# First q piece by SP's queue, doubled natural q and k tiles, a DMA-sharing schedule model and quotas of 10, 10, 10, 8, 7: sliding-window attention followed by a cosine-gated feed-forward layer

## The chip, the cores and the metric

The kernel runs on one core of one Trainium2 chip. The metric is the device time of one execution in microseconds (us). The kernel before was tuned already: 317.22 us, the median of three runs (317.15 to 318.24).

## The reference, cut to what matters

```python
batch, n_heads, seq, head_dim = (8, 8, 576, 64)          # q, k, v: float32
scores = scale * np.matmul(q, k.transpose(0, 1, 3, 2))
mask = (rel >= 0) & (rel < 128)                          # sliding window
scores = np.where(mask, scores + bias[None], -1e9)       # bias: ALiBi slopes
attn = softmax(scores); x = attn @ v                     # -> 4608 tokens x 512
h = x @ w_in                                             # 512 x 2048
g = h * np.cos(h)
return g @ w_out                                         # 2048 x 512
```

## The kernel before: the parts that matter

The kernel records operations, with what they read and write. A list scheduler with a model of durations then puts each engine's operations in an order. **The chip's time does not enter that model**: the model only decides the order. Waits on semaphores come from the recorded dependences.

Attention is cut into 72 units, 9 per batch: 8 of 256 queries of a head pair, and a tail. The feed-forward layer is cut into 9 chunks of 512 tokens. Phase c does the first matmul of chunk c, then `QUOTA[c]` attention units, then the second matmul of chunk c. The last units are thus far ahead of the chunk that uses them.

```python
QUOTA = [9, 9, 12, 12, 8, 8, 5]
...
# in schedule(), for an operation that issues a DMA: each queue has a wire of its own
if o.dma is not None:
    wire[e] = max(wire[e], st + 2300) + o.lat
    o.end = max(wire[e], st + o.occ + 1400) + 500
...
nat = {"q": sb("qnat", [128, NBLK, H, D]), "k": sb("knat", [128, NBLK, H, D])}   # one tile each
...
def load_nat(which, src, b):        # from batch 2 on: natural rows, 5 DMAs on GpSimd's queue
    ...
    op("pool", fns, w=[("nat", which)], dma=f"ldn{which}", occ=4400, lat=5500)

def dma_transposes(b):              # natural rows -> transposed rows, 2 DMAs on SP's queue
    for which in ("q", "k"):
        ...
        op("sp", fns, r=[("nat", which)] + ..., w=[("tr", which, b % 2)], ..., occ=2500, lat=6500)
...
# a finished unit is transposed into xT by PE if the next chunk needs it, else by a DMA from SP
first = (S * u[0] + (512 if u[1] == "t" else 256 * u[2])) // CH
after.append((first > phase + 1, u, ub, n))       # True: x_dma, False: x_pe
...
load_qk("q", q, 0, 0)               # all on GpSimd's queue, cast to bf16 by the DMA
load_qk("k", k, 0, 0)
distances()
identity()
load_qk("q", q, 0, 1)
load_qk("k", k, 0, 1)
constants()
load_v(0)
masks()
...
for u in range(4):
    load_w_in(u)
...
while next_t < B and done >= 9 * (next_t - 1):     # after the attention of a phase
    load_v(next_t)
    ...
    dma_transposes(next_t)
    next_t += 1
    if next_t < B:
        load_nat("q", q, next_t)
        load_nat("k", k, next_t)
```

Names: PE is TensorE, ACT ScalarE, DVE VectorE, POOL GpSimd, SP SyncE. `qrows` and `krows` are the rows of batches 0 and 1, `qnat` and `knat` the natural rows of later batches, `qt` and `kt` the transposed ones.

The softmax here doesn't subtract the row's maximum and nothing guards it: scores larger than these inputs give would overflow.

## Time and profile before

| | before |
|---|---|
| time, median of 3 (and of 6 in the comparison) | 317.22 us (317.75) |
| span of the profiled execution | 316.6 us; that execution took 318.35 us |
| PE busy | 303.8 us |
| matmuls that transpose x | 66 |
| PE wait for batch 4's transposed k | 1.3 us |

From the page of the kernel before (busy times; mean busy share of the DMA engines in tenths, 40 slices; shares of the chain that ended last):

```profile
span 316.6 us, 6278 instructions
...
PE 303.8 (96%) x2466; PEld 155.9 (49%) x2466; DVE 189.3 (60%) x453; ACT 202.9 (64%) x292; POOL 95.7 (30%) x123
...
DMA  6999999999999999999999994132013001201112
...
PE 84%; DMA 10%; POOL 4%; SPq 1%; issue 1%; ACT 0%; POOLq 0%; ACTq 0%
```

PE is the bound: there is little to win but its waits. The DMA engines are busy until slice 24 (190 us). The waits of PE (waiting line, what it waited for: total us, times, longest):

```profile
PE ps L432 <- DMA qrows<-in_q_dram: 5.8, 2, 5.4
PE ps L476 <- DMA kt<-knat: 1.3, 1, 1.3
PE ps L485 <- DVE kt L448: 0.9, 1, 0.9
...
PE ps L432 <- DMA krows<-in_k_dram: 0.4, 1, 0.4
```

The 5.4 us are the start. The 1.3 us are the one wait over 0.4 us after the first 15 us (one of 0.5 us, left out above, ends at 13.99). The chain of waits that leads to it (start us, duration us, what):

```profile
94.40 1.73 POOL knat L341 x2
96.13 6.68 DMA knat<-in_k_dram
102.83 1.87 SPq L350
...
104.74 8.81 DMA kt<-knat
...
113.59 0.41 PE ps L476 x16
```

Natural k is loaded until 102.8 us, transposed by a DMA until 113.55, and PE starts on it at 113.59. The start in the timeline (start, duration, engine, line, operation, and in brackets the idle time before and what ended it):

```profile
5.40 1.07 PE L432 MATMUL ps<-ident,qrows 128*64 128x128 bf16 x16 [5.40 <-DMA qrows<-in_q_dram]
6.91 1.07 PE L432 MATMUL ps<-ident,krows 128*64 128x128 bf16 x16 [0.44 <-DMA krows<-in_k_dram]
8.85 0.83 PE L485 MATMUL ps<-qt,kt 64*128 64x256 bf16 x8 [0.88 <-DVE kt L448]
```

### The profile page before, as it was taken

The page shows a single profiled execution, that of the slowest core. Times are in us where ns is not written, and L with a number is a line of the kernel's source. Part 1 is how long each engine was busy: PE and PEld are TensorE (multiplying, and loading weights), DVE is VectorE, ACT ScalarE, POOL GpSimd, SP SyncE. Part 2 cuts the span into 40 slices and gives each one's busy share as a digit, 9 for nine tenths or more (in the row PEclk, how much of TensorE's full clock was granted, in tenths as well). Part 3 has the DMA queues.
Part 4 walks back from the last instruction along what each step waited for, and adds up shares of the span by engine and source line. Part 5 has one row for each costly group of instructions (what it writes and reads, how often), then busy time and mean ns, then how long its engine had stood idle before and what let it go on. Part 6 is the DMA issues. An engine that isn't in the chain of part 4 may idle for free.

```text
span 316.6 us, 6278 instructions
## 1 busy us (share of the span) xinstructions
PE 303.8 (96%) x2466; PEld 155.9 (49%) x2466; DVE 189.3 (60%) x453; ACT 202.9 (64%) x292; POOL 95.7 (30%) x123
## 2 busy tenths in 40 slices
PE   2799999999999989999999999999999999999996
PEld 2577755444544554455444444454445444444444
DVE  2798858676685777858795856574753461363000
ACT  5896865886698766867787766667674553362211
POOL 8997140078357554564507200000000000000000
PEclk9999999999999999999999999999999999999999
DMA  6999999999999999999999994132013001201112
GB/s 95 178 206 210 205 161 192 154 154 133 172 175 165 164 157 158 171 168 183 155 126 122 163 111 85 66 77 58 18 56 73 33 0 48 86 0 68 66 72 94
DMA packets 144620, 37.82 MB, mean 119 GB/s; under 512 B 134224, under 2 KB 139600, under 8 KB 144592
## 3 DMA queue, kind: packets, MB, share of 16 engines
q0 software_dynamic: 99616, 18.36, 77.1%
q1 hardware_dynamic: 44976, 19.08, 29.8%
q8 instruction: 19, 0.31, 0.4%
q14 instruction: 9, 0.07, 0.1%
HBM read 36.70 MB, written 9.44 MB: 146 GB/s over the span
## 4 chain that ended last, share of the span: by engine, by line
PE 84%; DMA 10%; POOL 4%; SPq 1%; issue 1%; ACT 0%; POOLq 0%; ACTq 0%
PE ps L746 36%; PE ps L675 34%; DMA qrows<-in_q_dram 5%; PE ps L485 4%; DMA kt<-knat 3%; PE ps L570 2%; DMA knat<-in_k_dram 2%; PE ps L698 2%; PE ps L573 1%; POOL vp L331 1%; PE ps L720 1%; PE ps L639 1%; PE ps L432 1%; POOL w_inb L361 1%; PE ps L557 1%; PE ps L476 1%
## 5 line engine op out<-in xcount | busy, mean ns | idle before, releaser
L746 PE MATMUL ps<-w_outb,gT 128*128 128x512 bf16 x560 | 134.2, 380 | 0.0
L675 PE MATMUL ps<-xT,w_inb 128*128 128x512 bf16 x512 | 115.9, 379 | 0.0
L684 DVE TENSOR_TENSOR gT<-ps,cos 128x512 bf16<-128x512 f32 x128 | 81.0, 685 | 47.8 <-PE ps L746 39.0
L680 ACT ACTIVATE cos<-ps,halfpi 128x512 f32<-128x512 f32 x128 | 80.6, 688 | 31.1 <-PE ps L746 13.4
L746 PEld LDWEIGHTS ps<-w_outb,gT 128*128 128x128 bf16 x560 | 51.6, 98 | 56.4 <-issue 1.7
L675 PEld LDWEIGHTS ps<-xT,w_inb 128*128 128x128 bf16 x512 | 48.4, 97 | 57.4 <-DVE gT L684 4.5
L515 ACT ACTIVATE p<-ps 128x768 bf16<-128x768 f32 (+1 forms) x64 | 55.4, 915 | 22.0 <-PE ps L485 19.0
L539 DVE TENSOR_TENSOR p<-p,emask 128x512 bf16<-128x512 bf16 (+1 forms) x96 | 41.2, 460 | 8.0 <-ACT p L515 7.6
L752 ACT ACTIVATE ob<-ps 128x512 f32<-128x512 f32 x26 | 15.6, 599 | 38.7 <-PE ps L746 38.6
L331 POOL DMA_DIRECT2D vp<-in_v_dram x40 | 33.8, 882 | 15.3 <-issue 9.3
L341 POOL DMA_DIRECT2D qnat<-in_q_dram x30 | 25.3, 877 | 38.8 <-DMA qt<-qnat 38.8
L341 POOL DMA_DIRECT2D knat<-in_k_dram x30 | 25.3, 879 | 25.7 <-DMA kt<-knat 23.3
L611 DVE TENSOR_TENSOR xnat<-ps,rec 128x256 bf16<-128x256 f32 x64 | 24.4, 420 | 0.5
L485 PE MATMUL ps<-qt,kt 64*128 64x128 bf16 (+1 forms) x320 | 19.1, 245 | 1.7 <-DVE kt L448 0.9
L570 PEld LDWEIGHTS ps<-vp,p 128*128 128x128 bf16 x256 | 15.7, 97 | 7.4 <-issue 3.5
L570 PE MATMUL ps<-vp,p 128*128 128x65 bf16 x256 | 18.2, 194 | 0.4 <-issue 0.3
L485 PEld LDWEIGHTS ps<-qt,kt 64*128 64x128 bf16 x320 | 11.5, 96 | 12.8 <-issue 5.3
L609 DVE RECIPROCAL rec<-ps 128x4 f32<-128x4 f32 x64 | 8.2, 167 | 15.3 <-PE ps L573 14.9
L573 PE MATMUL ps<-vp,p 128*128 128x65 bf16 x192 | 17.0, 193 | 0.0
L698 PE MATMUL ps<-xT,w_inb 128*128 128x256 bf16 x128 | 16.2, 273 | 0.1
L573 PEld LDWEIGHTS ps<-vp,p 128*128 128x128 bf16 x192 | 13.3, 97 | 0.5
L754 DVE COPY ob<-ps 128x512 f32<-128x512 f32 x9 | 6.2, 691 | 12.2 <-PE ps L746 12.2
(52 smaller groups left out, 173.1 us busy)
## 6 DMA issues: line engine op xcount, KB each, us to landing
out_dram<-ob SPq DMA_DIRECT2D x35, 256.0 KB, 2.2
vp<-in_v_dram POOLq DMA_DIRECT2D x32, 128.0 KB, 9.0
qnat<-in_q_dram POOLq DMA_DIRECT2D x24, 128.0 KB, 5.7
knat<-in_k_dram POOLq DMA_DIRECT2D x24, 128.0 KB, 5.8
w_inb<-in_moe_w_in_dram POOLq DMA_DIRECT2D x4, 512.0 KB, 10.4
w_outb<-in_moe_w_out_dram POOLq DMA_DIRECT2D x4, 512.0 KB, 22.6
qrows<-in_q_dram POOLq DMA_DIRECT2D x1, 576.0 KB, 15.5
krows<-in_k_dram POOLq DMA_DIRECT2D x1, 576.0 KB, 17.6
```

The costliest lines, as they stand in the source:

```text
L331: op("pool", [lambda e, t=t, rows=rows: e.dma_start(vp[b % 2][0:rows, t, :, 0:64], v[b, :, 128 * t:128 * t + rows, :].rearrange("h p d -> ...
L341: fns.append(lambda e, t=t, rows=rows: e.dma_start(nat[which][0:rows, t, :, :], src[b, :, 128 * t:128 * t + rows, :].rearrange("h p d -> p ...
L485: ins = e.matmul(ps[:, banks[x], c0:c1], keys_ap(b, x, pr, kc), query_ap(b, x, pr, qb, 128 * nb), start=True, stop=True)
L515: op("act", lambda e: e.activation(P[i][:, :, 0:hi], src_[:, :, 0:hi], ACTF.Exp, scale=0.125), w=held + [("P", i)], occ=920 if G else 691, ...
L539: op("dve", lambda e, p=p, m=m: e.tensor_tensor(p, p, m, ALU.mult), r=[("P", i), ("EM", h0), ("EM", h1)], w=[("P", i)] if n != 1 else [("P ...
L570: ins = e.matmul(o, P[i][:, x, d0:d0 + 128], V[:, kc, h, 0:65], start=True, stop=not two)
L573: ins = e.matmul(o, P[i][:, x, p0:p0 + 128], V[:, kc - 1, h, 0:65], start=False, stop=True)
L611: op("dve", lambda e: e.tensor_tensor(o, U[:, :, :, 0:64], rv[:, :, :, None].broadcast_to([128, 2, 2, 64]), ALU.mult), r=[("rec", n % 2)], ...
L675: op("pe", lambda e, kc=kc: e.matmul(ps[:, bank, :], w_in[:, kc, 128 * fc:128 * fc + 128], xT[:, kc, r0:r0 + CH], start=(kc == 0), stop=(k ...
L680: op("act", lambda e: e.activation(cosb[ci][:, :], ps[:, bank, :], ACTF.Sin, bias=halfpi[:, 0:1]), r=["halfpi"], w=[("B", bank), ("cos", c ...
L684: op("dve", lambda e: e.tensor_tensor(gT[gi][:, fc, :], ps[:, bank, :], cosb[ci][:, :], ALU.mult), r=[("cos", ci)], w=[("B", bank), ("g", ...
L746: op("pe", lambda e, t=t, fc=fc, bank=bank: e.matmul(ps[:, bank, :], gT[gi][:, fc, 128 * t:128 * t + 128], w_out[:, fc, :], start=(fc == 0 ...
```

## The change

Its intent: to start earlier by using SP's idle queue for the first q piece; to let the natural loads of a batch begin while those of the batch before are still being transposed; to tell the scheduler that both queues share the DMA engines; and to spread the attention units more evenly over the phases.

```diff
-                wire[e] = max(wire[e], st + 2300) + o.lat
+                other = "sp" if e == "pool" else "pool"
+                begin = max(wire[e], st + 2300)
+                both = min(o.lat, max(0, wire[other] - begin))
+                wire[e] = begin + o.lat + both
+                wire[other] += both
...
-        nat = {"q": sb("qnat", ...), "k": sb("knat", ...)}
+        nat = {w_: [sb(f"{w_}nat{i}", ...) for i in range(2)] for w_ in ("q", "k")}
...
-        QUOTA = [9, 9, 12, 12, 8, 8, 5]
+        QUOTA = [9, 9, 10, 10, 10, 8, 7]
...
+        def load_first_q():
+            op("sp", [lambda e: e.dma_start(obuf[:, 0:2, :], rows)], ..., dma="hwq", ...)
+            for y, eng in enumerate(("dve", "act")):     # cast the float halves to bf16
+                op(eng, ..., r=[("ob", y)], w=[("qB", "q", 0, y)], ...)
...
-            op("pool", fns, w=[("nat", which)], dma=f"ldn{which}", occ=4400, lat=5500)
+            op("pool", fns, r=[("tr", which, 0)] if b == 3 else [], w=[("nat", which, b % 2)],
+               dma=f"ldn{which}{b % 2}", occ=4400, lat=4500)
...   # modelled latencies: DMA transposes 6500 -> 4300 and 500 -> 450, stores 600 -> 750
-        load_qk("q", q, 0, 0)
+        load_first_q()
         load_qk("k", k, 0, 0)
...
-        load_v(0)
+        load_v(0, range(2))
+        load_w_in(0)
+        load_v(0, range(2, NBLK))
```

More of the change, by code (lines that the diff above doesn't have):

```diff
@@ L267, in bass_alibi_sliding__then__act_gcu_kernel @@
         qB = {"q": sb("qrows", [128, 2, 1152]), "k": sb("krows", [128, 2, 1152])}
-        nat = {"q": sb("qnat", [128, NBLK, H, D]), "k": sb("knat", [128, NBLK, H, D])}
+        nat = {w_: [sb(f"{w_}nat{i}", [128, NBLK, H, D]) for i in range(2)] for w_ in ("q", "k")}
         tr = {w_: [sb(f"{w_}t{i}", [128, 2560]) for i in range(2)] for w_ in ("q", "k")}
@@ L280, in bass_alibi_sliding__then__act_gcu_kernel @@
         NOB = 4
-        ob = [sb(f"ob{i}", [128, 512], F32) for i in range(NOB)]
+        obuf = sb("ob", [128, NOB, 512], F32)
+        ob = [obuf[:, i, :] for i in range(NOB)]
         rec = [sb(f"rec{i}", [128, 8], F32) for i in range(2)]
@@ L317, in piece_keys @@
         def piece_keys(which, b, n):
-            return [("qB", which, 0), ("qB", which, 1)] if b else [("qB", which, n)]
+            keys = [("qB", which, 0), ("qB", which, 1)] if b else [("qB", which, n)]
+            return keys + ([("qB", "q", 0, 0), ("qB", "q", 0, 1)] if which == "q" and n == 0 else [])
         def load_qk(which, src, b, n=0):
@@ L326, in load_qk @@
                w=piece_keys(which, b, n), dma=f"ld{which}{n}", occ=740, lat=159 * R)
+        def load_first_q():
+            t0, R, _ = PIECES[0][0]
+            rows = bass.AP(q.tensor, q[0].offset, [[64 * R, 32], [64 * S, H], [1, 64 * R]])
+            op("sp", [lambda e: e.dma_start(obuf[:, 0:2, :], rows)],
+               w=[("ob", 0), ("ob", 1)], dma="hwq", occ=60, lat=500)
+            for y, eng in enumerate(("dve", "act")):
+                o = qB["q"][:, y, 0:512]
+                op(eng, (lambda e, o=o, y=y: e.tensor_copy(o, ob[y])) if y == 0 else
+                   (lambda e, o=o, y=y: e.activation(o, ob[y], ACTF.Copy)),
+                   r=[("ob", y)], w=[("qB", "q", 0, y)], occ=(340, 450)[y], lat=(420, 560)[y],
+                   pri=3)
         def load_v(b, order=range(NBLK)):
@@ L341, in load_nat @@
                 fns.append(lambda e, t=t, rows=rows: e.dma_start(
-                    nat[which][0:rows, t, :, :],
+                    nat[which][b % 2][0:rows, t, :, :],
                     src[b, :, 128 * t:128 * t + rows, :].rearrange("h p d -> p h d")))
-            op("pool", fns, w=[("nat", which)], dma=f"ldn{which}", occ=4400, lat=5500)
+            op("pool", fns, r=[("tr", which, 0)] if b == 3 else [], w=[("nat", which, b % 2)],
+               dma=f"ldn{which}{b % 2}", occ=4400, lat=4500)
         def dma_transposes(b):
@@ L351, in dma_transposes @@
                         t[:, 0:4, :, :].rearrange("p c k t -> p (c k) t"),
-                        nat[which][:, 0:4, :, :].rearrange("p c h d -> p (c h d)")),
+                        nat[which][b % 2][:, 0:4, :, :].rearrange("p c h d -> p (c h d)")),
                     lambda e, t=t, which=which: e.dma_start_transpose(
                         t[:, 4, :, 0:64],
-                        nat[which][0:64, 4, :, :].rearrange("p h d -> p (h d)")),
+                        nat[which][b % 2][0:64, 4, :, :].rearrange("p h d -> p (h d)")),
                 ]
-                op("sp", fns, r=[("nat", which)] + ([("ktail", b % 2)] if which == "k" else []),
-                   w=[("tr", which, b % 2)], dma=f"tr{which}{b % 2}", occ=2500, lat=6500)
+                op("sp", fns, r=[("nat", which, b % 2)] + ([("ktail", b % 2)] if which == "k" else []),
+                   w=[("tr", which, b % 2)], dma=f"tr{which}{b % 2}", occ=2500, lat=4300)
         def load_w_in(u):
@@ L658, in x_dma @@
                    r=[("xtl", b % 2)], w=[k_ for p_ in range(NPAIR) for k_ in xkeys(p_, t0, 64)],
-                   dma=f"xt{b % 2}", occ=1250, lat=500)
+                   dma=f"xt{b % 2}", occ=1250, lat=450)
                 return
@@ L663, in x_dma @@
                 xT[:, pr, t0:t0 + 256].rearrange("p (r t) -> p r t", r=2), xnat[n % NX][:, :])],
-               r=[("xnat", n % NX)], w=xkeys(pr, t0, 256), dma=f"x{n % NX}", occ=1250, lat=500)
+               r=[("xnat", n % NX)], w=xkeys(pr, t0, 256), dma=f"x{n % NX}", occ=1250, lat=450)
         ccount = [0]
@@ L752, in moe2 @@
                    {"act": lambda e, bank=bank, oi=oi: e.activation(
-                       ob[oi][:, :], ps[:, bank, :], ACTF.Copy),
-                    "dve": lambda e, bank=bank, oi=oi: e.tensor_copy(ob[oi][:, :], ps[:, bank, :])},
+                       ob[oi], ps[:, bank, :], ACTF.Copy),
+                    "dve": lambda e, bank=bank, oi=oi: e.tensor_copy(ob[oi], ps[:, bank, :])},
                    w=[("B", bank), ("ob", oi)], occ={"act": 490, "dve": 606},
@@ L758, in moe2 @@
                 op("sp", [lambda e, oi=oi, row=row: e.dma_start(out[row:row + 128, :],
-                                                                ob[oi][:, :])],
-                   r=[("ob", oi)], dma=f"st{oi}", occ=60, lat=600)
+                                                                ob[oi])],
+                   r=[("ob", oi)], dma=f"st{oi}", occ=330, lat=750)
         ucount = [0]
@@ L809, in bass_alibi_sliding__then__act_gcu_kernel @@
             qk_transposes(0, "k", n, 0, UB)
-        for u in range(4):
+        for u in range(1, 4):
             load_w_in(u)
```

## The prediction

> **What bounds the kernel.** TensorE (PE). The page gives PE 303.8 us of a 316.6 us span (96%) and a chain that ended last that is 84% PE, 10% DMA, 4% POOL. In the timeline of PE, 512-column matmuls start 216 ns apart in both feed-forward stages throughout. The waits view lists under 10 us: 5.8 us for q rows (5.4 before anything has begun, 0.38 at 28.8 us), 0.4 for the first k rows, 1.4 for k copies, and one steady stall, 1.3 us at 113.6 us, for batch 4's transposed k. So the change can win only at the start and at that stall; all else is PE work.
>
> **Start.** Before: POOL issues q at 1.32 us (0.82 us) and k at 2.15; they land at 5.36 and 6.87; the first scores start at 8.85. After: SP issues q, POOL issues k first, 0.8 us earlier, and all its later loads too. The Trainium skill ("DMA: Bandwidth & Descriptors", "Issuing engines are not separate DMA queues") says both queues share the same 16 engines, so the q bytes are not free; but they move before POOL's first bytes. I expect k landed near 5.5 us. New cost: two casts, an estimated 0.4 us on VectorE and 0.5 us on ScalarE, the latter after four mask exponentials (0.32 us each, from about 3.4 us): PE starts at about 5.3 us, as before, but k's transposes follow without their wait. First scores near 8.3 us. ScalarE is busy nearly without a break from 9.4 to 20.5 us, so that shift is kept. Batch 1's rows (landing at 28.72 and 31.51 us, in an always full DMA queue) land 0.8 to 1.5 us earlier, so the 0.38 us wait mostly goes. Worth 0.8 us in all.
>
> **Batch 4 stall.** The chain of waits shows k loads issued at 92.7 us, after batch 3's k transposes landed (92.1), landed at 102.8, transposed by 113.55. With two natural tiles these loads go out some 8 to 15 us earlier, and batch 4's first use comes later (10 units, not 12, in that phase). The stall goes: 1.3 us. POOL's waits for q and k transposes (38.8 and 23.3 us) shrink by more than half; that alone gains nothing.
>
> **Cost.** The new quotas make 7 more units be transposed on PE instead of by DMA (instruction order: 66 to 80 matmuls). A pair costs PE 0.11 us: 0.8 us more. Switches between score and other matmuls stay 38 groups. Fewer units in the fullest phases save perhaps 0.3 us of short waits for exponentials.
>
> **Sum.** -0.8 -1.3 -0.3 +0.8 = -1.6 us: 315.6 us. Range 313.7 to 317.2. Faster by over 2%: 0.02; within 2%: 0.96; slower: 0.02.
>
> **What would show it.** Right: first scores at 8.0 to 8.5 us; no PE wait over 0.3 us after 35 us; 80 identity transposes of x; PE busy 303 to 304 us. Wrong: k landing after 6.5 us (SP's q crowding it out); the ScalarE cast holding PE past 5.7 us; batch 2's transposes (landed 69.0, used 70.5 before: the tightest) late by sharing DMA; a new wait in phases 5 and 6, which got more units.
>
> **What would make it wrong.** Loads running ahead may slow the DMA transposes (4 to 10 us each, DMA busy 90% up to 190 us) enough to stall batch 2 or 3; then 317 to 319 us. If the earlier start carries through whole (1.5 us), 314.5.

## The result

The changed kernel took 318.39 us at the median of six runs (317.75 to 319.08), the kernel before in the same rounds 317.75 (317.15 to 318.6). The ratio is 1.0021, with a 95% interval of 0.9998 to 1.0045: the same time, and outside the predicted range of 313.7 to 317.2. The two profiled executions, 318.38 and 318.35 us, are also alike: after the change PE was busy 1.1 us longer and idle about as much less. All ratios here are the mean time of one kernel's fast runs over that of the other's fast runs of the same rounds, so not quite the ratio of the medians. Executions over 1.5% slower than the fastest of the same kernel are left out of the means.

The page of the changed kernel, the lines that answer to those above:

```profile
span 316.5 us, 6268 instructions
...
PE 304.9 (96%) x2480; PEld 155.9 (49%) x2480; DVE 188.5 (60%) x448; ACT 209.5 (66%) x306; POOL 95.1 (30%) x122
...
DMA  7999999999999999999999894320012001201112
...
PE 62%; DMA 18%; POOL 11%; SPq 6%; issue 1%; ACT 0%; POOLq 0%; ACTq 0%
```

PE is as full as before, with 1.1 us more of busy time. The chain that ended last now runs through DMA, POOL and SP for a third of the span. The waits of PE:

```profile
PE ps L454 <- ACT qrows L344: 5.8, 1, 5.8
PE ps L507 <- DVE kt L470: 0.9, 1, 0.9
PE ps L498 <- DMA kt<-knat: 0.6, 1, 0.6
```

The stall for batch 4's k is still there, and PE starts 0.36 us later than before. The chain that leads to the stall:

```profile
79.58 18.01 DMA qnat<-in_q_dram
...
97.60 4.98 SPq L372
...
104.59 7.36 SPq L372
...
112.00 6.59 DMA kt<-knat
...
118.63 0.41 PE ps L498 x16
```

The natural loads were issued 8.5 us (q) and 12.4 us (k) earlier than before, as forecast. Yet the last of q's took 18.0 us to land, the large transposes of q and k then took SP 5.0 and 7.4 us to issue, and k landed transposed at 118.58 us, five microseconds later than in the trace before. The start, in the timeline:

```profile
5.04 0.63 ACT L344 ACTIVATE qrows<-ob 128x512 bf16<-128x512 f32 x1 [0.17 <-DMA ob<-in_q_dram]
...
5.76 1.06 PE L454 MATMUL ps<-ident,qrows 128*64 128x128 bf16 x16 [5.76 <-ACT qrows L344]
...
6.58 1.09 PE L454 MATMUL ps<-ident,krows 128*64 128x128 bf16 x16
...
8.55 0.82 PE L507 MATMUL ps<-qt,kt 64*128 64x256 bf16 x8 [0.88 <-DVE kt L470]
```

SP issued q at 0.81 us, but it landed only at 5.01; the two casts took 0.62 and 0.63 us where I had put 0.4 and 0.5 (the trace of before has ScalarE copies of 128x512 at 0.57 and 0.60 us). First scores came 0.30 us earlier than in this trace of before, not 0.55. Both traces happen to be late at the start: in a second trace of the changed kernel (e13) q landed at 4.73 us, PE started at 5.43 and first scores at 8.23. The transposes of x on PE, in the groups of instructions before:

```profile
L639 PE MATMUL ps<-ident,xnat 128*128 128x128 bf16 x66 | 8.8, 222 | 0.3
```

and after:

```profile
L661 PE MATMUL ps<-ident,xnat 128*128 128x128 bf16 x80 | 11.0, 222 | 0.0
```

POOL's waits are where the doubled tiles show. Before, its longest two:

```profile
POOL qnat L341 <- DMA qt<-qnat: 38.8, 5, 18.0
POOL knat L341 <- DMA kt<-knat: 23.3, 5, 11.7
```

and after, it waits for the attention to free v tiles instead:

```profile
POOL vp L351 <- PE ps L595: 37.8, 5, 13.3
POOL qnat L361 <- DMA qt<-qnat: 18.4, 1, 18.4
```

### The profile page after: what moved, and what is told of

Its sections match the earlier page's. It is cut to its first block, busy times and chain, and to the rows that moved or that the text cites. A ratio compares the mean times of both kernels' runs of the same rounds, so it can differ in the third digit from the quotient of the medians.

```text
span 316.5 us, 6268 instructions
## 1 busy us (share of the span) xinstructions
PE 304.9 (96%) x2480; PEld 155.9 (49%) x2480; DVE 188.5 (60%) x448; ACT 209.5 (66%) x306; POOL 95.1 (30%) x122
## 4 chain that ended last, share of the span: by engine, by line
PE 62%; DMA 18%; POOL 11%; SPq 6%; issue 1%; ACT 0%; POOLq 0%; ACTq 0%
PE ps L768 28%; PE ps L697 26%; DMA qnat<-in_q_dram 14%; SPq L372 6%; POOL vp L351 4%; POOL qnat L361 3%; PE ps L507 2%; DMA qt<-qnat 2%; DMA kt<-knat 2%; PE ps L592 2%; POOL knat L361 1%; PE ps L742 1%; POOL w_outb L389 1%; PE ps L595 1%; POOL w_inb L383 1%
## 5 line engine op out<-in xcount | busy, mean ns | idle before, releaser
L706 DVE TENSOR_TENSOR gT<-ps,cos 128x512 bf16<-128x512 f32 x128 | 81.9, 686 | 42.2 <-PE ps L768 29.8
L702 ACT ACTIVATE cos<-ps,halfpi 128x512 f32<-128x512 f32 x128 | 81.6, 688 | 29.2 <-PE ps L697 16.1
L774 ACT ACTIVATE ob<-ps 128x512 f32<-128x512 f32 x28 | 16.8, 599 | 41.8 <-PE ps L768 41.7
L361 POOL DMA_DIRECT2D qnat<-in_q_dram x30 | 25.6, 910 | 25.8 <-DMA qt<-qnat 18.4
L670 ACT ACTIVATE xT<-ps 128x256 bf16<-128x256 bf16 x27 | 9.9, 387 | 6.6 <-PE ps L661 6.5
## 6 DMA issues: line engine op xcount, KB each, us to landing
qnat<-in_q_dram POOLq DMA_DIRECT2D x24, 128.0 KB, 12.4
```

Of the source, the lines that this page charges most:

```text
L361: fns.append(lambda e, t=t, rows=rows: e.dma_start(nat[which][b % 2][0:rows, t, :, :], src[b, :, 128 * t:128 * t + rows, :].rearrange("h p ...
L702: op("act", lambda e: e.activation(cosb[ci][:, :], ps[:, bank, :], ACTF.Sin, bias=halfpi[:, 0:1]), r=["halfpi"], w=[("B", bank), ("cos", c ...
L706: op("dve", lambda e: e.tensor_tensor(gT[gi][:, fc, :], ps[:, bank, :], cosb[ci][:, :], ALU.mult), r=[("cos", ci)], w=[("B", bank), ("g", ...
```

## The experiments

The change has four parts: F (first q piece by SP, and the first w_in piece moved ahead of three v pieces), N (two natural tiles), M (the new model and latencies) and Q (quotas). Keeping none of them from the changed source gave exactly the instruction order of the kernel before, on every engine. All runs below were correct against the reference. A call is a set of kernels timed in the same rounds on one chip, the kernel before among them: e1 to e4, e5 to e8, e9 to e12, e13 to e15, e16 to e18. The runs of the kernel before scatter, so a comparison within one call says most. Medians are of all six runs. In its trace, e2 has the same instruction order as the kernel before on all five engines.

### One part alone, and all but one

**e1: F alone.** The only edit over the kernel before is part F of the diff.

> Kernel before plus the first part alone (first q piece by SP's queue into a float tile, two casts; first w_in piece moved ahead of three v pieces). Theory: in the changed kernel the start gained only 0.30 us (first scores 8.85 to 8.55) because q by SP landed no earlier than 5.01 and had to be cast; so 0.3 to 0.5 us faster here, stall of batch 4 (1.3 us) unchanged. Rival: the start was worth the predicted 0.8 us and something else ate it: first scores by 8.3 and 0.8 us faster.

Measured: 317.47 us (one slow run among the six, 322.31) against 318.17 for before, ratio 0.9989 (0.9934 to 1.0045). First scores at 8.24 us, and no wait for batch 4's k in this execution. The time can't tell 0.3 from 0.8 us. That the stall was gone was not foreseen: the first hint that the stall is not a fixed property of the kernel before.

**e2: N alone.** Two natural tiles and nothing else; old quotas, old model.

> Kernel before plus the doubled natural q and k tiles alone (old quotas, old model). Theory: the DMA engines are full, so loads issued earlier land hardly earlier and the loads of batch 5, now free to go, share the engines with batch 4's k transposes; those land at 113 to 119 us against 113.55 before, while their first use stays at 112 to 113 us: the stall stays at 1.3 us or grows to as much as 5 us; 0 to 4 us slower. Rival (my prediction): loads 8 to 15 us earlier, stall gone, 1.3 us faster.

Measured: 323.58 us, ratio 1.0173 (1.0129 to 1.0216). The wait of PE:

```profile
PE ps L493 <- DMA kt<-knat: 4.5, 1, 4.5
```

Batch 4's k landed at 116.91 us, against 113.55 in the trace of before. The rival was my prediction, and it fell: the doubled tiles alone make the stall three times as long. The time grew by 5.4 us, more than the wait. All six runs had a mean granted clock of 0.989 to 0.995; in the trace it was 0.5 for 3.4 us, from 116.3 to 119.7, as the wait ended.

**e3: Q alone.** `QUOTA = [9, 9, 10, 10, 10, 8, 7]` in the kernel before.

> Kernel before plus the new quotas alone. Theory: 80 x transposes on PE instead of 66 cost 0.8 us; batch 4 is first used about 4 us later (near 117 us) while its k lands at 113.5 as before, so the stall of 1.3 us goes: net 0.3 to 0.6 us faster. Rival: the later use is not what helped, the stall stays over 0.6 us and the kernel is 0.2 to 0.8 us slower.

Measured: 318.57 us, ratio 1.0001 (0.9947 to 1.0055). Two of the six runs were slow (322.94 and 323.73, clocks 0.995 and 0.989); the median of the other four is 317.57. Its trace, of a fast run, has no wait for batch 4's k, which landed at 109.06 and was first used at 112. So the use was not 4 us later, as I had written: that later use in the changed kernel comes from the new model's order, not from the quotas. The net gain did not show.

**e4: all but Q.** The changed kernel with `QUOTA = [9, 9, 12, 12, 8, 8, 5]`.

> The changed kernel with the old quotas. Theory: k of batch 4 lands near 118 us as in the changed kernel (118.58) but is wanted near 113: a stall of 3 to 5 us, less the 0.8 us of x transposes saved: 1 to 4 us slower than before. Rival: doubled tiles serve the old quotas too; stall under 1 us, and 0.8 us faster than the changed kernel.

Measured: 316.97 us (316.65 to 317.32), ratio 0.9969 (0.9924 to 1.0013), span 314.9 us. My theory fell here. K landed at 117.5 us, late as expected, but the new model had put batch 4's first scores at 118.0 us and filled the time before with other matmuls, so nothing waited. Only parts F and M lie between e2 and e4, and F alone (e1) did not move batch 4's first use later (110.8 us in its trace): the order that the model makes is what makes doubled tiles bearable. The interval includes 1, so e4 alone does not show a gain over the kernel before, and the other parts were not left out one at a time.

### Does the kernel before always stall?

**e5: the kernel before again**, unchanged.

> The kernel before, unchanged, as a run of its own. Its times so far fall in two groups, 316.5 to 317.4 and 318.2 to 319.1 us. Theory: the batch-4 stall (1.3 us in the one trace, k landed at 113.55) is not in every execution, since that landing hangs on a chain of DMAs with no slack; again two groups, and a ratio within 0.3% of 1. Rival: the stall is in every execution, one group.

Measured: 318.25 us (316.6 to 318.78) beside the same kernel's 317.63; ratio 1.0018 (0.9993 to 1.0042). This is a kernel against itself: a ratio of 1.002 is what this measurement gives for no difference. Its trace has no wait for batch 4's k (landed at 110.83), but another one that the first trace lacks:

```profile
PE ps L698 <- DMA w_inb<-in_moe_w_in_dram: 1.2, 1, 1.2
```

**e16 and e17: the kernel before**, one execution each.

> The kernel before, one look. Theory (fast and slow executions of it differ by stalls for DMAs that land with no slack): if its span is under 315.7 us, its trace has neither a wait of 0.6 us or more for batch 4's k nor one for a w_in piece near 18 us; if over 316.3, it has at least one. Rival: the two groups differ in something else, and a short execution has such a wait too.

> The same once more: same rule by span, under 315.7 us no such wait, over 316.3 us at least one.

Measured: 317.43 us with a span of 315.7, and 317.88 us with 316.1. Neither span fell on a decided side of my rule, but the size of the wait answers. In e16:

```profile
PE ps L476 <- DMA kt<-knat: 0.4, 1, 0.4
```

and in e17:

```profile
PE ps L476 <- DMA kt<-knat: 0.7, 1, 0.7
```

The four traces of this kernel have waits for batch 4's k of 1.3, 0, 0.4 and 0.7 us. Taking the stall of each (for e5 the 1.2 us for w_in) from its execution time leaves 317.05, 317.23, 317.03 and 317.18 us. So a stall of 0 to 1.3 us for a DMA without slack accounts for most of the difference between the first trace, e16 and e17. For e5 the agreement is partly chance, as its page shows (granted clock, in tenths, in 40 slices):

```profile
PEclk9979999999999999999999999999999999999999
```

The clock was 0.5 from 18.7 to 22.1 us, just after the wait for w_in. Eleven matmuls of 256 columns took 2.29 us there, against 1.36 in e16, and PE was busy for 304.9 us in all instead of 303.8. A wait can thus cost more than its length. That the wait brings the drop is inferred from their order, here and in e2 and e6; the 1.3 us wait of the first trace was not followed by one. Of 69 executions of the kernel before, 37 took less than 317.6 us, 24 took 317.6 to 319.3 and 8 took 320 to 322.3; the last eight were never traced. All eight have a mean granted clock of 0.995, as e5's traced execution has, so each lost clock too; which wait came before it stays open.

**e18: only the first w_in piece moved forward** in the kernel before.

```diff
-        load_v(0)
+        load_v(0, range(2))
+        load_w_in(0)
+        load_v(0, range(2, NBLK))
```

> Kernel before with only the first w_in piece moved ahead of three v pieces. Theory: it takes away the wait for w_in near 18 us that one of two traces of the kernel before has (1.2 us), but not that for batch 4's k: median 0 to 0.8 us below before, some executions still over 318 us. Rival: no effect, within 0.2 us of before at the median.

Measured: 317.43 us (317.02 to 317.86) against 316.97, ratio 1.0005 (0.9961 to 1.005). There is no gain: the median is 0.46 us above that of before, and the ratio is 1 within its noise, so the theory fell; the rival's 0.2 us is missed too, upwards. None of its six runs was over 318 us, which six runs can't establish as an effect.

### Do loads that run ahead slow the transposes?

The edit that holds them back, the same in e6, e7, e8 and later: q and k loads of batch 5 and on wait until the k transposes of the batch before have landed. Batch 4's loads stay early.

```diff
-            op("pool", fns, r=[("tr", which, 0)] if b == 3 else [],
+            op("pool", fns, r=[("tr", "k", (b - 1) % 2)] if b >= 5 else [("tr", which, 0)] if b == 3 else [],
```

**e6: N alone, held.**

> Doubled natural tiles alone as in e2, but q and k loads of batch 5 and later wait until the k transposes of the batch before have landed; order on TensorE, ScalarE, VectorE and GpSimd as in e2. Theory (loads of batch 5 share the DMA engines with batch 4's transposes and halve their pace): batch 4's k lands at 107 to 112 us against 116.9 in e2, the 4.5 us stall goes, 3 to 5 us faster than e2 and within 1 us of before. Rival (the loads of batch 4 themselves or the later SP order delay it): k lands after 114, stall over 1.5 us.

Measured: batch 4's k landed at 110.94 us (116.91 in e2) and the 4.5 us wait was gone, as the theory said. But the kernel took 326.45 us, ratio 1.0291 (1.0261 to 1.0321), because of a new wait further on (and the granted clock was 0.5 for 6.8 us, from 157.6 to 164.5, around its end):

```profile
PE ps L693 <- DVE xnat L629: 7.5, 1, 7.5
```

The view names VectorE, but the transposed x came by DMA, and SP's queue was late. SP in the timeline:

```profile
141.98 0.52 SPq L776 DMA_DIRECT2D out_dram<-ob  x1
146.43 5.39 SPq L368 DMA_TRANSPOSE qt<-qnat  x1
151.87 1.26 SPq L371 DMA_TRANSPOSE qt<-qnat  x1
153.18 1.24 SPq L680 DMA_TRANSPOSE xT<-xnat  x1
```

The old model had put q transposes of batch 6 ahead of two x transposes in SP's order. The held loads landed at 146.41 us, SP stood until then, and those x transposes landed at 160.02 and 160.23; PE went on at 160.52. The Trainium skill ("DMA: Bandwidth & Descriptors", "Anatomy of one DMA — SWDGE (gpsimd) path") says that DMA engines do not wait on semaphores, the issuing sequencer does; this trace agrees: SP issued nothing from 142.5 to 146.43 us.

**e7: the changed kernel, held.** Only SP's order differs from the changed kernel's; PE, ACT, DVE and POOL keep theirs.

> The changed kernel with the same hold on loads of batch 5 and later; only SP's order differs. Theory: batch 4's k lands by 114 us (118.58 in the changed kernel), the 0.65 us stall goes, 0.4 to 0.8 us faster than the changed kernel, unless v loads behind the held ones come late (then a wait for v near 140 us). Rival: stall of 0.5 us or more stays.

**e8: the changed kernel with old quotas, held.**

> The changed kernel with the old quotas and the hold. e4 (old quotas, no hold) had no stall at all, because the new model put batch 4's first scores at 118 us. Theory: so the hold has nothing to win: within 0.3 us of e4 (0.997 of before). Rival: 0.5 us or more faster than e4.

Measured: e7 317.76 us (317.38 to 317.98), ratio 1.001 (0.9993 to 1.0027); e8 316.46 us (316.42 to 316.79), ratio 0.9972 (0.9956 to 0.9989). In e7 k landed at 112.84 us and PE did not wait for it, and no wait for v appeared. SP's order up to these transposes is the same in both traces, which rules out the order as a cause. While k was transposed in e7, POOL issued no load at all (v loads queue behind the held ones). So the competition for the DMA engines is the cause of the late landing: the hold alone moved it by 5.7 us, 0.6 of them by an earlier start of the transposes and 5.1 by their pace (8.9 us from issue to landing, against 14.0). e8 is clear of the kernel before by 0.3%, and near e4 by its ratio, as expected (the medians differ by 0.5 us). They were run at other times. Between e7 and e8 only the quotas (and the order that follows from them) differ: 1.3 us.

The sharing shows in the packets of the trace. In the changed kernel between 110.5 and 113.0 us, SP's queue (transposes, mostly k of batch 4) moved 708 packets and 192 KB, POOL's 703 packets and 89 KB: 77 GB/s for the transposes. In e7 between 109.0 and 112.5 us SP's queue had the engines alone and moved 164 GB/s. The Trainium skill ("DMA: Bandwidth & Descriptors", "Queues, rings and completion order") says that each DMA engine takes turns between queues, packet by packet. The equal packet counts agree with it (687 and 685 in the same stretch of e13): while both queues have work, an early load that nobody needs yet gets every second packet. Whether one packet of the trace is one packet of the page is not shown.

### The terms one by one

**e9: e8 with 7 more units transposed by PE**, in the phases in which the new quotas do so.

```diff
-                        after.append((first > phase + 1, u, ub, n))
+                        by_dma = first > phase + 1
+                        if by_dma and u[1] != "t" and extra.get(phase, 0) > 0:   # {3: 2, 4: 2, 5: 1, 6: 2}
+                            extra[phase] -= 1
+                            by_dma = False
+                        after.append((by_dma, u, ub, n))
```

> e8 (old quotas, hold) with 7 more units transposed on TensorE, in the same phases as the new quotas would (80 instead of 66 matmuls), nothing else asked for. Theory: 14 matmuls of 55 ns: 0.6 to 1.0 us slower than e8, that is 0.999 to 1.001 of before. Rival (these transposes are hidden, it is the quotas' balance that costs): within 0.2 us of e8.

**e10: e8 with the first q piece by POOL's queue** and no casts.

> e8 with the first q piece by GpSimd's queue and no casts, as before; the w_in piece stays ahead of the v pieces. Theory: first scores 0.3 us later (8.85), 0.2 to 0.5 us slower than e8. Rival: the SP load is worth the predicted 0.8 us: 0.7 us or more slower.

**e11: e8 with single natural tiles** (and so no hold).

> Old quotas, first q piece by SP, new model, but single natural tiles (no hold needed). Theory: the doubled tile is worth nothing here, as k of batch 4 lands by 113 us with single tiles too and its scores stand later: within 0.3 us of e8, no stall over 0.3 us after 35 us. Rival: doubled tiles are what keeps e4 and e8 free of stalls: a stall of 1 us or more, 1 us slower than e8.

**e12: e8 with quotas 9, 9, 12, 10, 10, 8, 5**, which need PE for no more units than the old ones (25 in the phases that the quotas rule, against 32 with the new).

> e8 with quotas 9, 9, 12, 10, 10, 8, 5: as flat as the new ones from the fourth phase on, but with no more transposes on TensorE than before (66). Theory: flatness itself neither costs nor gains: within 0.4 us of e8. Rival: flat phases cost time by themselves: 0.7 us or more slower than e8; or they gain: 0.5 us faster.

Measured, with before at 318.52 us:

| kernel | median us (range) | ratio to before (95%) |
|---|---|---|
| e9, 80 transposes | 317.34 (317.10 to 317.69) | 0.9963 (0.9925 to 1.0002) |
| e10, q by POOL | 316.73 (316.22 to 316.97) | 0.9940 (0.9901 to 0.9978) |
| e11, single tiles | 316.99 (316.76 to 317.17) | 0.9949 (0.9907 to 0.9991) |
| e12, 12, 10, 10, 8, 5 | 316.38 (316.23 to 316.55) | 0.9931 (0.9893 to 0.9969) |

Fourteen more transposes cost 0.9 us over e8 (316.46, from the other call): the predicted 0.8 us was right, and they are not hidden. e12 serves as a check: it differs from e8 in quotas alone, and against it e9, e10 and e11 are 0.96, 0.35 and 0.61 us slower. Taking q by POOL again costs 0.3 us over e8: SP's load of q is worth that much and not 0.8; first scores at 8.47 us against 8.29. With single tiles k landed at 113.2 us, no wait over 0.3 us, and the kernel was 0.5 us slower than e8, more than the 0.3 I had allowed and less than the rival's 1; so doubled tiles, once held back and scheduled with the new model, may be worth half a microsecond. Flat quotas as such cost nothing that shows: e12 is as fast as e8. They were run at other times.

### The last question: how much is the stall, how much the quotas?

**e13, e14, e15**: the changed kernel, the same with the hold (e7), and the same with the hold and quotas 9, 9, 12, 10, 10, 8, 5 (e12), again, on one chip in the same rounds.

> The changed kernel again, same chip and rounds as its held version and the flat quotas with 66 transposes. Theory: its trace again has batch 4's k landing after 117 us and a PE wait of 0.3 to 1.5 us for it; time within 0.4% of before. Rival (its stall was a chance of one execution, as with the kernel before): k lands by 115 us, no wait.

> e7 again, beside e13 on the same chip. Theory: 0.4 to 0.9 us faster than e13, k of batch 4 landing by 114 us, no wait. Rival: same time as e13 within 0.2 us.

> e12 again (the only edit over e14 is quotas 9, 9, 12, 10, 10, 8, 5), beside e14. Theory: 14 transposes fewer, 0.7 to 1.4 us faster than e14, 1.3 to 2.2 us faster than e13, and faster than before clear of noise. Rival: the gap to e14 is under 0.4 us.

Measured, with before at 317.00 us at the median:

| kernel | median us (range) | k of batch 4 landed | PE wait for it |
|---|---|---|---|
| e13, changed | 317.79 (317.37 to 318.63) | 118.81 | 0.7 |
| e14, held | 317.59 (317.45 to 317.83) | 112.13 | none |
| e15, held, 66 transposes | 316.63 (316.41 to 317.49) | 112.05 | none |

SP in the timeline of the changed kernel, transposing batch 4's k while POOL's loads of batch 5 run:

```profile
104.59 7.36 SPq L372 DMA_TRANSPOSE kt<-knat  x1
112.00 1.30 SPq L375 DMA_TRANSPOSE kt<-knat  x1
```

and in e14, the same two transposes with those loads held:

```profile
103.83 4.67 SPq L373 DMA_TRANSPOSE kt<-knat  x1
108.53 1.84 SPq L376 DMA_TRANSPOSE kt<-knat  x1
```

The stall is in both traces of the changed kernel (0.6 and 0.7 us), and the hold removes it in both of its own. The profiled executions show that in their spans (316.8 against 316.0 us), but the timed medians differ by only 0.2 us, short of the 0.4 that I expected. How large the stall is in untraced executions stays open. The transposes' term is firm: 0.96 us between e14 and e15 at the medians, 0.81 at the means. The ratios to before were 1.0000 (0.9951 to 1.0049), 0.9998 (0.9954 to 1.0042) and 0.9973 (0.9928 to 1.0018); they are wide because a run of before took 321.4 us and lifts its mean.

The best version is thus the changed kernel with the hold and either old quotas (e8) or 9, 9, 12, 10, 10, 8, 5 (e12, e15): 316.4 to 316.6 us, ratios 0.9972, 0.9931 and 0.9973. The first two are clear of noise, the third is not, though it is the same kernel as the second.

## Why the prediction was wrong, point by point

| term | predicted | what the runs showed |
|---|---|---|
| start | -0.8 | -0.3 (e10 against e8 and e12), against first scores 0.2 to 0.3 us earlier |
| batch 4's stall | -1.3 | about 0: before 1.3, 0, 0.4, 0.7 (mean 0.6); after 0.6, 0.7 |
| short waits for exponentials | -0.3 | none seen: 0.3 before, 0.3 after in the waits of PE |
| x transposes on PE | +0.8 | +0.9 to +0.96 (e9 against e8 and e12), +0.96 with the quotas (e15 to e14) |
| sum | -1.6 | +0.6 by these terms; measured +0.64 and +0.79 at the medians, but ratios of 1.0021 and 1.0000, neither clear of noise |

The range and the size were wrong; "within 2%" was right.

**The step that failed** is "The stall goes: 1.3 us". In its place, the changed kernel still has a stall of 0.6 and 0.7 us in its two traces, as much as the 0.6 us that four traces of before have in the mean. The step failed twice over.

First, in the base. The 1.3 us was read from one execution that took 318.35 us, and it was taken off a median of 317.22 us. An execution of 317.2 us has little of that stall: e16 at 317.43 had 0.4 us of it. The median could not lose what it did not have. The same holds for the first scores: in the three other traces of before they start at 8.45, 8.51 and 8.48 us, and the 8.85 of the first trace was the slow one.

Second, in the mechanism. "With two natural tiles these loads go out some 8 to 15 us earlier" came true (8.5 and 12.4 us), but the loads did not land earlier by that: natural k of batch 4 landed at 100.67 us against 102.81. The DMA engines were full, as I had read from the page, and I did not carry this through. A queue that waits less at its head only stands longer in the pipe. The loads of batch 5, released too, then took every second packet from the transposes of batch 4. My paragraph "What would make it wrong" named this, for batches 2 and 3; e2, e6 and e7 show it, for batch 4.

**The start** had the right sign. Its failed step is what I drew from "they move before POOL's first bytes", "I expect k landed near 5.5 us": q did move first (packets from 2.33 to 4.67 us), but POOL's k, issued at 1.33 us, then got its first packet at 4.26 us, 2.9 us after its issue; before, q's first packet had come 1.5 us after its issue on the same queue. So k landed at 6.21 us, not 5.5 (5.88 to 6.10 in the ten other traces with q on SP's queue). The casts were longer than estimated, and "the ScalarE cast holding PE past 5.7 us", which I had listed as a sign against me, came true in that trace (5.76), but not in e13 (5.43). Moreover the rows of batch 1 landed only 0.74 us earlier (27.98 against 28.72), so PE, itself earlier, still waited 0.3 us for them (0.8 us in e13): the DMA stream sets this point, not the first scores.

**What held.** The cost of the transposes and their number (80); the 38 groups of score matmuls; POOL's waits for transposes (62.1 us before, 18.4 after), which gained nothing; no new wait in the last phases; batch 2, the tightest, did not stall. PE busy, forecast at 303 to 304 us, was 304.9.

**What the quotas do.** They move seven units into phases whose next chunk needs them at once, so PE has to transpose them. This is arithmetic on the rule `first > phase + 1`, and it could have been counted for other quotas before any was chosen: 9, 9, 12, 10, 10, 8, 5 is nearly as flat and needs none of the seven.

## What to carry to other kernels

A stall read from one profiled execution may only be taken off the time of that same execution; compare the execution's own time with the median, and look at more than one trace before a stall of a microsecond is counted as a gain. Where DMA is full, a second buffer lets work without urgency compete with work that is waited for, and then a dependence that holds the early loads back, with a schedule order that knows of the sharing, is what helped here (e8, e12). A wait of PE may also come with a lower granted clock and so cost more than its length (e2, e5, e6): look at the clock of the execution. Before changing quotas in a phased schedule, count what the change moves onto the engine that bounds the kernel.

## What the Trainium skill lacked or had wrong

- "DMA: Bandwidth & Descriptors", table of specifications, gives a first-byte latency of about 1 us for GpSimd's queue and 0.6 us for SP's. In these traces the first packet came 1.5 us after the start of the issue on both: SP 0.81 to 2.33 us, POOL 1.32 to 2.86 us. The issue itself (0.73 and 0.82 us) is included; counted from its end it is 0.79 and 0.71 us, so the page's difference between the queues does not show here either way. The page does not say where it counts from.
- No page says that a software queue's first packets can be kept back while another queue's load is in flight: POOL's first packet came 2.7 to 2.9 us after its issue in the eleven traces with SP's q load beside it, 1.5 us in the nine without. Why is not shown. "Issuing engines are not separate DMA queues" says only that they interleave.
- "Queues, rings and completion order" has the packet-by-packet turns right (703 and 708 packets in 2.5 us), but not what follows for a kernel: the DMA transposes fell from 164 to 77 GB/s beside plain loads, and the large transpose of one natural tile took SP 7.4 us to issue beside loads all the way, 4.7 and 5.3 us (e14, e7) where the loads ended before it did.
